# Queries and keys by Strassen's block product in the first stage of a fused attention and feed-forward kernel

## The chip, the cores and the metric

The kernel runs on one core of a Trainium2 chip, in one launch. The metric is the device time of one execution in microseconds. The profile gives, beside it, the span from the first to the last instruction of one profiled execution, which is a little shorter.

The engines: TensorE (PE; PEld is its loading of weights) multiplies, VectorE (DVE), ScalarE (ACT) and GpSimd (POOL) do the elementwise work, and SyncE (SP) issues nearly all transfers. Each has a queue of its own. SBUF is the memory on the chip, in 128 partitions; PSUM holds the matmul results, in banks of 512 float32 per partition.

## The reference

`x` is 2048 tokens by 640 features. It is normalised per token without scale or shift, and the result goes into an attention and a two-layer feed-forward part whose outputs are multiplied:

```python
xn = _layernorm(x, axis=-1)
s = _A_ref(xn, A_wqkv, A_wo)
g = _silu(_B_ref(xn, B_w1, B_b1, B_w2, B_b2))
return x + s * g
```

`_A_ref` forms queries, keys and values (`xn @ wqkv`, 640 by 1920) for 32 heads of 20 features. A token attends to itself and the 255 tokens before it, with a softmax; the outputs of all heads go through `wo`. `_B_ref` is `relu(xn @ w1 + b1)` squared, times `w2`, plus `b2`, with 1536 inner features.

## The kernel before

**High and low parts.** Every operand of a product is held as a high part in float32r, rounded by a ScalarE copy, and a low part, what the rounding left, made by a VectorE or GpSimd subtract. A product is the sum of three matmuls: high by high, low by high, high by low. The 640 features are 5 chunks of 128 (`KC`), the tokens 4 blocks of 512 (`NB`, `BT`). One group of 128 query or key features for one token block takes 5 x 3 = 15 matmuls of 512 columns.

**First stage** (L138 to L410). For each block the tokens are normalised, turned (`transpose_chunks`) and split into `xT`; the block's values are formed (`v_all`, two halves of four tiles, three banks in turn) and stored; the group-0 queries and keys of each block are formed with full matmuls (`qk_group`, L210) and stored (`qk_evac`, `qk_stores`). A stored query or key has three parts: two times the high and once the low part, so that one score matmul of 60 rows holds the three products.

**Main stage** (L1218 on). It goes through 16 head pairs with 16 key tiles each, in 267 steps. In a step, `scores` (L483) multiplies a query tile by its keys, for two heads, into the two banks of the pool `pat`; `maxima` (L491) takes row maxima with VectorE and so frees these banks; nine steps later (`LAG`) `scores_t` (L523) and `exps` (L529) make the exponentials, GpSimd masks them, and two steps after that (`PLAG`), for eight tiles together, `values` (L561) multiplies them by the values: a burst of 48 or 72 small matmuls. Between these stands the filler: a generator that hands out the remaining work a matmul at a time, as halves of 64 rows that run beside each other (L471, line L473 in the profile). Its order is: queries and keys of groups 1 to 4 for all blocks (`order_qk`, 32 products), then for two halves of the inner features and the four blocks the hidden layer (`hps`) and the second layer (`yps`), and after the last step the output product (`wops`, L627).

**What sets the order.** Both stages run under a schedule written by hand: each engine's queue takes the instructions in the order of the program, SyncE's among them, so an instruction that waits holds all behind it on its engine. In the main stage a planned clock (`COST` in microseconds for each matmul, `burst_cost`) decides how much filler stands between two steps: `total` sums all planned work, and `pace` is `total` less a surplus for the bursts, per step. `due[s]` is when step s is planned. A step does its scores, fills up to `due[s] + EARLY_FILL * pace`, and then either fills up to `due[s + 1]` or, in a burst step, runs the burst:

```python
fill(due[s] + EARLY_FILL * pace)
...
if r:
    fill(due[s + 1] - burst_cost(r))
    values(e[0], r)
else:
    fill(due[s + 1])
```

Raw weights come through a ring of three tiles (`wraw`, `RAW`), in the main stage by `piece`, `tick` and `issue`.

## Time and profile before

| | us |
|---|---|
| median of 3 runs | 843.65 (843.51 to 843.78) |
| the profiled execution | 843.45 |
| its span, first to last instruction | 841.7 |
| TensorE busy in the span | 832.2 |
| VectorE busy | 460.4 |
| ScalarE busy | 423.8 |
| GpSimd busy | 333.5 |

A row of a group in the profile names the line, the engine, the operation, what it writes and reads with shapes, and the count; then the busy time in us, the mean of one in ns, and the idle time of the engine just before them with what ended it. A piece of the chain or of the timeline has its start and its length in us. "x30" means 30 instructions merged. A matmul's own duration is longer than its distance to the next, since they are pipelined.

### The profile page before, as it was taken

To read this page: it belongs to the slowest core of one execution; us is meant where nothing else is said; L and a number is where in the kernel's file an instruction comes from. 1 tells how busy PE (TensorE), PEld (TensorE's weight loads), DVE (VectorE), ACT (ScalarE), POOL (GpSimd) and SP (SyncE) were. 2 spreads that over 40 slices of the span, in tenths; PEclk is the share of its full clock that TensorE was granted. 3 is DMA by queue.
4 is the path that set the end of the run, shared out by engine and by line. 5 is a ranking of instruction groups with operands and counts; after the bars stand their busy time and mean duration, and the time that the engine had idled before them with its cause. 6 is when DMAs were issued, how large, how long until landed. Compare 5 with 4: busy or idle time off the path is not lost.

```text
span 841.7 us, 25475 instructions
## 1 busy us (share of the span) xinstructions
PE 832.2 (99%) x10176; PEld 782.1 (93%) x10176; DVE 460.4 (55%) x1370; ACT 423.8 (50%) x792; POOL 333.5 (40%) x652
## 2 busy tenths in 40 slices
PE   8999999999999999999999999999999999999997
PEld 8999999888888999999999999899999999999997
DVE  7643126666567745455455476654445455446764
ACT  6232104545466763664653765744654755663321
POOL 5110001434333553553553553643543644552543
PEclk9999999999999999999999999999999999999999
DMA  7998488879989456345256354486365365266962
GB/s 253 288 393 331 157 205 252 267 240 278 299 267 288 144 175 176 97 163 156 80 183 193 91 147 141 125 248 197 85 223 170 83 208 189 59 187 207 385 202 79
DMA packets 89774, 166.42 MB, mean 198 GB/s; under 512 B 10424, under 2 KB 38200, under 8 KB 88632
## 3 DMA queue, kind: packets, MB, share of 16 engines
q1 hardware_dynamic: 89496, 164.64, 62.3%
q8 instruction: 80, 1.31, 0.7%
q14 instruction: 38, 0.31, 0.1%
q10 hardware_dynamic: 160, 0.16, 0.1%
HBM read 93.66 MB, written 70.52 MB: 195 GB/s over the span
## 4 chain that ended last, share of the span: by engine, by line
PE 94%; issue 1%; POOL 1%; ACT 1%; DVE 1%; DMA 1%; SPq 0%; DVEq 0%; POOLq 0%
PE yps L473 21%; PE hps L473 20%; PE qkps L473 14%; PE ops L561 10%; PE wops L627 8%; PE vps L233 8%; PE stps L523 5%; PE sps L483 4%; PE qkps L210 2%; POOL wv L189 1%; PE tps L177 1%; DMA raw<-in_A_wqkv_dram 1%; DVE junk L491 0%; ACT p L529 0%; ACT relu L977 0%
## 5 line engine op out<-in xcount | busy, mean ns | idle before, releaser
L491 DVE CUSTOM_DVE_ANT_0 junk<-sps,mask 128x384 bf16<-128x384 f32 (+2 forms) x512 | 272.3, 532 | 257.7 <-PE sps L483 81.5
L529 ACT ACTIVATE p<-stps 128x768 f32<-128x768 f32 (+2 forms) x256 | 197.4, 771 | 246.2 <-PE stps L523 202.5
L530 POOL TENSOR_SCALAR_AFFINE_SELECT p<-p 128x256 f32<-128x256 f32 x256 | 109.9, 429 | 320.5 <-ACT p L529 315.3
L473 PE MATMUL yps<-w,hh 64*128 64x320 f32 x1536 | 226.1, 309 | 0.8 <-ACT relu L977 0.8
L473 PE MATMUL hps<-xb,w 64*128 64x256 f32 (+1 forms) x2100 | 212.0, 304 | 0.0
L473 PEld LDWEIGHTS hps<-xb,w 64*128 64x128 f32 x2100 | 194.6, 187 | 3.9 <-issue 2.7
L473 PEld LDWEIGHTS yps<-w,hh 64*128 64x128 f32 x1536 | 184.2, 185 | 4.1 <-ACT relu L977 1.6
L473 PE MATMUL yps<-w,hl 64*128 64x320 f32 x768 | 175.3, 308 | 0.0
L483 PE MATMUL sps<-ks,qs 60*128 60x384 f32 (+2 forms) x512 | 132.4, 335 | 0.6 <-DVE mt L491 0.5
L523 PE MATMUL stps<-qs,ks 62*128 62x384 f32 (+2 forms) x512 | 128.0, 333 | 0.2 <-ACT row L504 0.2
L473 PEld LDWEIGHTS yps<-w,hl 64*128 64x128 f32 x768 | 117.8, 185 | 1.1 <-issue 1.0
L473 PE MATMUL qkps<-xT,wgkh 64*128 64x512 f32 x320 | 100.3, 394 | 0.0
L473 PE MATMUL qkps<-xT,wgqh 64*128 64x512 f32 x320 | 98.5, 392 | 0.0
L532 POOL TENSOR_SCALAR_AFFINE_SELECT p<-p 128x256 f32<-128x256 f32 x224 | 95.6, 427 | 0.0
L561 PE MATMUL ops<-p,vp 128*21 128x128 f32 (+1 forms) x2128 | 86.9, 311 | 0.0
L483 PEld LDWEIGHTS sps<-ks,qs 60*128 60x128 f32 x512 | 82.5, 185 | 4.6 <-DVE mt L491 2.2
L561 PEld LDWEIGHTS ops<-p,vp 128*21 128x21 f32 x2128 | 63.8, 100 | 21.2 <-issue 6.3
L523 PEld LDWEIGHTS stps<-qs,ks 62*128 62x128 f32 x512 | 81.8, 187 | 0.9 <-ACT row L504 0.6
L233 PE MATMUL vps<-wv,xT 128*128 128x320 f32 x480 | 71.9, 309 | 0.8 <-POOL wv L189 0.8
L233 PEld LDWEIGHTS vps<-wv,xT 128*128 128x128 f32 x480 | 70.5, 187 | 1.3 <-POOL wv L189 1.0
L982 POOL TENSOR_TENSOR hl<-sq,hh 128x512 fp32r<-128x512 f32 x48 | 62.1, 1294 | 16.4 <-ACT sq L981 16.3
L627 PE MATMUL wops<-wo,oT 128*128 128x320 f32 x384 | 61.9, 310 | 0.0
(104 smaller groups left out, 1167.7 us busy)
## 6 DMA issues: line engine op xcount, KB each, us to landing
ks<-k_d SPq DMA_DIRECT2D x64, 240.0 KB
qs<-q_d SPq DMA_DIRECT2D x64, 240.0 KB
xb<-xs SPq DMA_DIRECT2D x60, 256.0 KB
xs<-xT SPq DMA_DIRECT2D x8, 1280.0 KB
k_d<-shm SPq DMA_DIRECT2D x19, 512.0 KB
q_d<-shm SPq DMA_DIRECT2D x19, 512.0 KB
y<-ysb SPq DMA_DIRECT2D x28, 320.0 KB
o<-osb SPq DMA_DIRECT2D x64, 128.0 KB
```

Source lines behind the costliest of these rows:

```text
L210: nc.tensor.matmul(ps, wt[:, c, :], xT[part][b][:, c * BT + t0:c * BT + t0 + n], start=m == 1, stop=m == 3 * KC)
L233: nc.tensor.matmul(ps, xT[xp][b][:, c * BT + t * P: c * BT + (t + 1) * P], wv[wp][:, c, nh * HALF:(nh + 1) * HALF], start=first and m == 0 ...
L473: return nc.tensor.matmul(out, a[r], b_[r], skip_group_check=True, **kw)
L483: nc.tensor.matmul(ss[hh][:, :nk], qs[i][o, q * P:(q + 1) * P], ks[i][o, k0 * P:k0 * P + nk], start=True, stop=True)
L491: nc.vector.tensor_tensor_reduce(out=junk[:, :nk], in0=ss[hh][:, :nk], in1=mask[:, 3 * P - nk:], scale=1.0, scalar=-3.0e38, op0=ALU.add, o ...
L523: nc.tensor.matmul(tps[:, hh, :n], ks[i][o, kb * P:(kb + 1) * P], qs[i][o, kb * P:kb * P + n], start=True, stop=True)
L529: nc.scalar.activation(p32[:, :, :n], tps[:, :, :n], AF.Exp, scale=SCALE)
L530: nc.gpsimd.affine_select(p32[:, :, 0:P], p32[:, :, 0:P], pattern=[[0, 2], [1, P]], compare_op=ALU.is_ge, fill=0.0, base=0, channel_multip ...
L532: nc.gpsimd.affine_select(p32[:, :, 2 * P:], p32[:, :, 2 * P:], pattern=[[0, 2], [-1, P]], compare_op=ALU.is_gt, fill=0.0, base=0, channel ...
L561: nc.tensor.matmul(ot[r0:r0 + VW, c0:c0 + len(part), :], vps[p][:, kb // 4, kb % 4, hh, :], pt[:, hh, :].rearrange("p (t n) -> p t n", n=P ...
L627: nc.tensor.matmul(ps, a, b_, start=j == 0, stop=j == n - 1)
L982: nc.gpsimd.tensor_sub(hh[1][:, :BT], sq, f32(hh[0]))
```

## The change

Queries and keys of groups 1 to 4 leave the filler, and group 0 of blocks 2 and 3 leaves the first stage's direct way. They are formed in nine passes after the values. A pass takes one group of 128 features and two token blocks. The 2 by 2 block product (query and key rows by two blocks, the features cut into chunks 0, 1 and 3, 4, with chunk 2 multiplied directly) is done with seven products instead of eight, from sums of weights and sums of tokens, each split into high and low parts. The four results come from sums in the banks and copies of them.

The token sums of blocks 0 and 1 are made in `v_all(2)` by GpSimd, the first pass's weights in `v_all(3)`. In a pass, the next pass's weights, the token sums of blocks 2 and 3 (passes 1 to 4) and the rounding of the first half of `w1` (passes 5 to 7) are dealt out between the products by `aside`. The raw weights for the pass after the next are loaded at the end of a pass.

Queries and keys are stored in two parts, one store for each result, and the loads of a head pair repeat the high part: two transfers for each of the four tiles instead of one. In the main stage the filler begins with the hidden layer, with `w1`'s first half already there, and `total` has no term for queries and keys.

```diff
-    qk_d = {w: dram.tile([D, NPART, S], F32, name=f"{w}_d") for w in "qk"}
-
-    def qk_stores(w, rows, cols, hi, lo):
-        dst = qk_d[w][rows, :, cols]
-        twice, once = (slice(0, 3, 2), 1) if w == "q" else (slice(0, 2), 2)
-        return [(dst[:, twice, :], f32(hi).unsqueeze(1).to_broadcast([P, 2, hi.shape[-1]])), (dst[:, once, :], f32(lo))]
+    qk_d = {w: dram.tile([D, 2, S], F32, name=f"{w}_d") for w in "qk"}
+
+    def qk_store(w, rows, cols, both):
+        return (qk_d[w][rows, :, cols], f32(both))
...
-                r.append((f32(st[p % 2])[h * HP:h * HP + KR, cols], qk_d[w][src, :, cols].rearrange("d a n -> (d a) n")))
+                dst = f32(st[p % 2])[h * HP:h * HP + KR, cols]
+                two = qk_d["q"][src, :, cols].rearrange("d a n -> (d a) n") if w == "q" else qk_d["k"][src, 0, cols].unsqueeze(1).to_broadcast([DH, 2, HS])
+                r += [(dst[0:2 * DH], two), (dst[2 * DH:], qk_d[w][src, int(w == "k"), cols])]
...
+    PASSES = [(j, g) for j in range(2) for g in range(KC) if j or g]
+    passed, sums_of, graws = {}, {}, deque()
+
+    def load_raws():
+        k = len(graws) + len(passed)
+        if k < len(PASSES):
+            graws.append({w: load_w(group_src(PASSES[k][1], w), KC) for w in "kq"})
+
+    def weight_jobs(slots, spare):
+        k = len(passed)
+        hi, lo = ([slots(4 * a + j).rearrange("p (c n) -> p c n", n=P) for j in range(4)] for a in range(2))
...
+        raw = graws.popleft()
+        q_, k_ = raw["q"], raw["k"]
+        s14 = spare()[:, :4 * P].rearrange("p (c n) -> p c n", n=P)
+        s23 = wgt.tile([P, D], F32, tag="wraw", bufs=RAW, name="s23").rearrange("p (c n) -> p c n", n=P)
+        s1, s4 = s14[:, 0:2], s14[:, 2:4]
+
+        def rounded(j, cs, src):
+            return [lambda: nc.scalar.activation(hi[j][:, cs], src, AF.Copy), lambda: nc.gpsimd.tensor_sub(lo[j][:, cs], src, f32(hi[j][:, cs]))]
+
+        def add(dst, a, b_, sub=True):
+            return [lambda: (nc.vector.tensor_sub if sub else nc.vector.tensor_add)(dst, a, b_)]
+        cs = slice
+        return [rounded(0, cs(0, 5), q_),
+                add(s1, k_[:, 0:2], k_[:, 3:5], False),
+                rounded(1, cs(0, 3), k_[:, 2:5]),
+                add(s23[:, 0:2], s1, q_[:, 0:2]),
+                rounded(1, cs(3, 5), s1),
+                add(s23[:, 2:5], q_[:, 0:3], k_[:, 0:3]),
+                add(s4, q_[:, 3:5], s23[:, 0:2]),
+                rounded(2, cs(0, 5), s23),
+                rounded(3, cs(0, 2), s4)]
+
...
+    def token_jobs(j, tiles, mixed, room, parts):
+        sums_of[j] = t = halves_of(tiles)
...
+            one, two = part, slice(3 + part.start, 3 + part.stop)
+            (h0, l0), (h1, l1) = views
+            jobs += [op(True, 1, h1[:, one], h0[:, one]), op(False, 1, 1, l1[:, one]), op(True, 1, 1, l0[:, one]),
+                     op(True, 2, h1[:, two], 1), op(False, 2, 2, l1[:, two]), rounded(1),
+                     op(True, 4, h0[:, two], 2), op(False, 4, 4, l0[:, two]), rounded(2),
+                     op(True, 3, h1[:, two], h1[:, one]), rounded(4), op(False, 3, 3, l1[:, two]), op(True, 3, 3, l1[:, one]), rounded(3)]
+        return jobs
+
...
-            jobs = norm_jobs(b + 2) if b + 2 < NB else []
+            jobs = norm_jobs(b + 2) if b + 2 < NB else ahead_jobs[b]
...
-                    for _ in range(0 if between and not nh else 2 if between else 1):
+                    for _ in range(0 if between and not nh else 2 if between else 1 if b + 2 < NB else 2):
                         if jobs:
-                            jobs.pop(0)()
+                            run(jobs.pop(0))
...
-                for w in "kq":
-                    ps = mm_bank([P, BT], "qkps")
-                    qk_group(w, b, ps)
-                    qk_evac(w, b, ps)
+                if b == 1:
+                    for w in "kq":
+                        ps = mm_bank([P, BT], "qkps")
+                        qk_group(w, b, ps)
+                        qk_evac(w, b, ps)
                 next_x()
...
+                if b == 2:
+                    lots = [at.tile([P, S], F32R, tag=w, name=f"t_{w}") for w in ("qs0", "ks0")] + [ptt.tile([P, S], F32R, tag=f"t{i}", name=f"t_{i}") for i in range(2)]
+                    ahead_jobs[2] = token_jobs(0, lots, (), lambda: p1b.tile([P, 2, BT], F32, tag="shl", bufs=3, name="acc"), [slice(0, 2)])
+                if b == 3:
+                    ahead_jobs[3] = weight_jobs(even_slots(), lambda: p1b.tile([P, D], F32, tag="xn", name="s14"))
+                v_all(b)
+            store_all()
+            load_raws()
+
+    with tc.tile_pool(name="ph1b", bufs=1) as p1c:
+        seat = [0]
+        homes = [(pmm, "mm0"), (pmm, "mm1"), (pmm, "mm2"), (pat, "s"), (pat, "s"), (p1t, "s"), (p1t, "s"), (po_, "o")]
+
+        def bank():
+            pool, tag = homes[seat[0] % 8]
+            seat[0] += 1
+            return pool.tile([P, BT], F32, tag=tag, name="gps")
+
...
+        def copy_of(ps):
+            m = p1c.tile([P, BT], F32, tag="m", bufs=3, name="m")
+            nc.scalar.activation(m, ps, AF.Copy)
+            return m
+
+        with tc.manual_schedule(engines={E_.PE, E_.Activation, E_.DVE, E_.Pool, E_.SP}):
...
+            for i, (j, g) in enumerate(PASSES):
+                hi, lo = passed[i]
+                blocks = (2 * j, 2 * j + 1)
+                X = [[xT[p][b].rearrange("p (c n) -> p c n", c=KC) for p in range(2)] for b in blocks]
+                T = sums_of[j]
+                a, b_, c, d = (bank() for _ in range(4))
+                begun = set()
+
+                def products(ps, slot, cs, right):
+                    for n, k in enumerate(cs):
+                        for wp, xp in ((0, 0), (1, 0), (0, 1)):
+                            nc.tensor.matmul(ps, (hi, lo)[wp][slot][:, k], right(xp, n), start=id(ps) not in begun, stop=True, skip_group_check=True)
+                            begun.add(id(ps))
+
+                def rows(blk, *chunks):
+                    return lambda xp, n: X[blk][xp][:, chunks[n]]
+
+                def summed(k):
+                    return lambda xp, n: T[k][xp][:, n]
+
+                def result(w, blk, ps, m):
+                    pair = p1c.tile([P, 2, BT], F32R, tag="c", bufs=3, name="c")
+                    nc.vector.tensor_add(f32(pair[:, 1]), ps, m)
+                    nc.scalar.activation(pair[:, 0], f32(pair[:, 1]), AF.Copy)
+                    nc.vector.tensor_sub(pair[:, 1], f32(pair[:, 1]), f32(pair[:, 0]))
+                    dst, src = qk_store(w, slice(g * P, (g + 1) * P), slice(blocks[blk] * BT, (blocks[blk] + 1) * BT), pair)
+                    nc.sync.dma_start(dst, src)
+
+                def aside(n):
+                    for _ in range(n):
+                        if side:
+                            run(side.popleft())
+                if i + 1 < len(PASSES):
+                    side.extend(weight_jobs(odd_slots() if i % 2 == 0 else even_slots(), lambda: p1c.tile([P, 4 * P], F32, tag="s14", name="s14")))
+                if i == 0:
+                    lots = [p1c.tile([P, S], F32R, tag=f"t{k}", name=f"t_{k}") for k in range(4)]
+                    later_jobs = deque(token_jobs(1, lots, (4, 5, 6, 7), lambda: p1c.tile([P, 1, BT], F32, tag="acc", bufs=3, name="acc"), [slice(0, 1), slice(1, 2)]))
+                if i == KC - 1:
+                    w1_first = Tiles("w1_0")
+                    for cc in range(3):
+                        w1_load(cc)
+                    later_jobs.extend(f for cc in range(3) for f in w1_jobs(cc))
+                if i == KC:
+                    for cc in range(3, KC):
+                        w1_load(cc)
+                    later_jobs.extend(f for cc in range(3, KC) for f in w1_jobs(cc))
+                    qs.append(at.tile([P, S], F32R, tag="qs0", name="qs0"))
+                    ks.append(at.tile([P, S], F32R, tag="ks0", name="ks0"))
+                    ones_rows(0)
                     for half in range(2):
                         for dst, src in pair_loads(0, half):
                             nc.sync.dma_start(dst, src)
-                v_all(b)
-            store_all()
+                for k in range(8 if i < KC - 1 else 2):
+                    if later_jobs:
+                        side.insert(min(len(side), 1 + 2 * k), later_jobs.popleft())
+                per = -(-len(side) // 6)
+                products(a, 0, (0, 1), rows(0, 0, 1))
+                m1 = copy_of(a)
+                aside(per)
+                products(b_, 0, (3, 4, 2), rows(0, 3, 4, 2))
+                result("q", 0, b_, m1)
+                aside(per)
+                products(c, 1, (3, 4), summed(1))
+                products(c, 1, (0,), rows(1, 2))
+                m5 = copy_of(c)
+                aside(per)
+                products(a, 2, (0, 1), summed(2))
+                u2 = copy_of(a)
+                aside(per)
+                products(d, 1, (1, 2), summed(4))
+                products(d, 1, (0,), rows(0, 2))
+                aside(per)
+                products(a, 2, (2, 3), summed(3))
+                u3 = copy_of(a)
+                result("k", 0, d, u3)
+                result("k", 1, a, m5)
+                aside(per)
+                products(c, 3, (0, 1), rows(1, 3, 4))
+                products(c, 2, (4,), rows(1, 2))
+                result("q", 1, c, u2)
+                aside(len(side))
+                if i + 2 < len(PASSES):
+                    load_raws()
+            while later_jobs:
+                run(later_jobs.popleft())
...
-    total = (8 * (KC - 1) * 15 * COST[BT] + 2 * NB * (15 * (WIDE * COST[BT] + 2 * (NFH - WIDE) * COST[MT]) + 8 * 18 * COST[HALF]) + NP * 2 * NT * COST[3 * P] + sum(burst_cost(r) for p in range(NP) for r in bursts(p)))
+    total = (2 * NB * (15 * (WIDE * COST[BT] + 2 * (NFH - WIDE) * COST[MT]) + 8 * 18 * COST[HALF]) + NP * 2 * NT * COST[3 * P] + sum(burst_cost(r) for p in range(NP) for r in bursts(p)))
...
-                    assert made_for(p + 1, 0)
-                    loads = [bulk_dma(0.7, *l) for l in pair_loads(p + 1, 0)]
+                    loads = [bulk_dma(0.35, *l) for l in pair_loads(p + 1, 0)]
```

In a part left out, the first sums on `token_jobs`' list go to GpSimd, except those with the numbers in `mixed` (4 to 7 for blocks 2 and 3), which go to VectorE; `rounded` there is a ScalarE copy and a VectorE subtract. `w1_load` brings a chunk of `w1`, and `w1_jobs` rounds it with ScalarE and subtracts with VectorE.

191 lines of the change are left out of this document (92 added, 99 removed).

## The prediction

> **What bounds the kernel now.** I read the page's busy shares first, then the chain of work that ended last, then that chain in order of time.
>
> ```profile
> span 841.7 us, 25475 instructions
> PE 832.2 (99%) x10176; PEld 782.1 (93%) x10176; DVE 460.4 (55%) x1370; ACT 423.8 (50%) x792; POOL 333.5 (40%) x652
> PE 94%; issue 1%; POOL 1%; ACT 1%; DVE 1%; DMA 1%; SPq 0%; DVEq 0%; POOLq 0%
> PEclk9999999999999999999999999999999999999999
> ```
>
> TensorE is busy 99% and is 94% of the chain, at full granted clock throughout. So fewer matmuls are worth their time, as long as nothing else makes TensorE wait.
>
> ```profile
> 66.66 6.87 PE qkps L210 x30
> 93.32 6.86 PE qkps L210 x30
> 100.18 17.59 PE vps L233 x120
> 118.03 2.36 PE qkps L473 x10
> 767.28 69.87 PE wops L627 x475
> ```
>
> These pieces of the chain give the stages: the first stage ends at 117.8 us (100.18 + 17.59); attention with its filler runs to 767.3, 649.5 us; the output product follows. One 128x512 matmul costs 6.87 / 30 = 0.229 us.
>
> **The matmuls.** What goes from the main stage is 960 half matmuls, 480 whole ones:
>
> ```profile
> L473 PE MATMUL qkps<-xT,wgkh 64*128 64x512 f32 x320 | 100.3, 394 | 0.0
> L473 PE MATMUL qkps<-xT,wgqh 64*128 64x512 f32 x320 | 98.5, 392 | 0.0
> L473 PE MATMUL qkps<-xT,wgql 64*128 64x512 f32 x160 | 61.4, 392 | 0.0
> L473 PE MATMUL qkps<-xT,wgkl 64*128 64x512 f32 x160 | 61.2, 391 | 0.0
> ```
>
> Their means overlap, so I price them by the stage: the planner's own costs (COST, and `total` at L1224) sum to 628.8 for a stage that took 649.5 us, a ratio of 1.033. Its term for queries and keys is 8 x 4 x 15 x 0.23 = 110.4, so 114.0 us go (bounds: 480 x 0.229 = 109.9, and 14% of the chain, 118). From the first stage go the group-0 products of blocks 2 and 3: 6.87 + 6.86 = 13.7. What comes is nine passes. In the diff a pass has 6 + 9 + 9 + 6 + 9 + 6 + 9 = 54 matmuls of 512 columns where the direct way has 60: 12.4 us a pass, 486 x 0.229 = 111.3 in all. The balance is 111.3 - 114.0 - 13.7 = **-16.4 us**, which is all that the change can bring. The rest asks what TensorE newly waits for.
>
> **The passes.** The side engines work by these rows:
>
> ```profile
> L904 ACT ACTIVATE shm<-qkps 128x512 fp32r<-128x512 f32 x32 | 18.8, 589 | 13.8 <-PE qkps L473 12.6 <-PE sps L483 0.9
> L907 DVE TENSOR_TENSOR slo<-qkps,shm 128x512 fp32r<-128x512 f32 x32 | 22.0, 687 | 7.4 <-ACT shm L904 7.4
> L815 ACT ACTIVATE w<-raw 128x640 fp32r<-128x640 f32 x12 | 8.8, 730 | 2.6 <-DMA raw<-in_B_w_dram 2.6
> L567 ACT ACTIVATE osb<-ops 128x256 f32<-128x256 f32 x64 | 21.9, 385 | 0.0
> L189 POOL TENSOR_TENSOR wgql<-raw,wgqh 128x640 fp32r<-128x640 f32 x2 | 3.4, 1718 | 27.6 <-ACT wgqh L188 27.6
> L982 POOL TENSOR_TENSOR hl<-sq,hh 128x512 fp32r<-128x512 f32 x48 | 62.1, 1294 | 16.4 <-ACT sq L981 16.3
> ```
>
> By them ScalarE has 8 x 0.59 (four bank copies, four high parts) plus 2,176 columns of weight rounding (some 2.8) = 7.5 us of a 12.4 us pass, and VectorE 8 x 0.69 plus 1,152 columns of weight sums (some 1.6) = 7.1. They fit; order is the question, since each queue runs in program order. A result is three dependent pieces, VectorE add, ScalarE copy, VectorE subtract: 0.69 + 0.59 + 0.69, about 2.07 with the handovers. Three stand at the end of a pass in one row (k0, k1, q1). The copy that opens the row can start 1.9 us before the pass's last matmul ends and takes 0.6; so q1 is ready -1.3 + 3 x 2.07 = 4.9 us into the next pass. SyncE is in order too: it waits for q1's store, and behind that stand the loads of the two raw weights, which ScalarE needs right after the *next* pass's first bank copy. Landing times, from the SyncE issue and the ScalarE piece that a weight load released:
>
> ```profile
> 271.28 0.46 SPq L803 DMA_DIRECT2D raw<-in_B_w_dram  x1
> 275.50 0.74 ACT L815 ACTIVATE w<-raw 128x640 fp32r<-128x640 f32 x1 [1.37 <-DMA raw<-in_B_w_dram]
> 275.63 0.33 SPq L803 DMA_DIRECT2D raw<-in_B_w_dram  x1
> 278.18 0.74 ACT L815 ACTIVATE w<-raw 128x640 fp32r<-128x640 f32 x1 [1.24 <-DMA raw<-in_B_w_dram]
> ```
>
> That is 4.2 us with other transfers about and 2.6 without. I take 3.7, near the busier one, since a 512 KB store and the other weight go ahead. The query weight, second to be loaded, is issued at 4.9 + 0.4 + 0.5 = 5.8 and lands 9.5 us into the pass. Until then ScalarE stands before the rounding of that weight, and behind it stand the q0 copy, one rounding, the m5 copy, another rounding and the u2 copy: 0.73 + 0.59 + 0.5 + 0.59 + 0.39 + 0.59 = 3.4 us. The u2 copy must have read bank `a` before its third products, due after 39 matmuls, at 8.9 us. TensorE waits 9.5 + 3.4 - 8.9 = 4.0 us. Seven passes (the second to the eighth) load so: **+28** (20 to 32 by the two landings; 0 if ScalarE gets there earlier than I count).
>
> The first four passes also carry the token sums of blocks 2 and 3 (12 GpSimd pieces of about 1.29 us, 16 VectorE and 8 ScalarE pieces), and passes five to seven the rounding of the first half of w1. A ScalarE piece that waits for a chain of GpSimd sums holds the next bank copy. Nothing before shows this order, so I bound it. In the first pass GpSimd needs 1.7 + 1.0 for two weight remainders and 3 x 1.29 for the first sum after the raw weight lands; VectorE's next sum and, behind a weight sum, ScalarE's next rounding stand behind that, so u3 comes some 5 us late and with it the second pass's raw weights; fading over three passes, 11 us. A w1 piece puts some 0.8 of ScalarE and a VectorE subtract ahead of q0: 3 to 4 a pass, 10 in all. The ends are 0, if the sums run ahead, and 21; I take **+10**, the middle. GpSimd has 2,176 columns a pass (5.5 us) and 12 x 1.29 / 4 of sums, 9.4 together.
>
> Two engines that read the same memory slow each other in this trace:
>
> ```profile
> 742.08 0.41 POOL L530 TENSOR_SCALAR_AFFINE_SELECT p<-p 128x256 f32<-128x256 f32 x1 [1.79 <-ACT p L529]
> 744.13 0.92 POOL L530 TENSOR_SCALAR_AFFINE_SELECT p<-p 128x256 f32<-128x256 f32 x1
> 743.19 2.53 DVE L825 TENSOR_TENSOR wo<-raw,wo 128x640 fp32r<-128x640 f32 x2 [0.76 <-ACT wo L824]
> ```
>
> The same select takes 0.41 us alone and 0.92 beside VectorE subtracts of two SBUF operands. [...]
>
> **Before the passes.** In the value products of block 2, GpSimd gets ten token sums of 1,024 columns, about 2.5 us each (2 x 1.29). It can begin only behind the memset that waits for a store:
>
> ```profile
> 70.91 0.24 POOL L241 MEMSET vt<- 128x64 f32 x1 [11.77 <-DMA v_d<-vt]
> ```
>
> From 71.2 they end near 96.4. ScalarE's rounding of the last sum (about 1.0) stands ahead of its copy of the block's last value bank, which is then read at 97.8. That bank is due for the third tile of the next value block, at (100.18 - 13.7) + 2 x 2.2 = 90.9 (17.59 / 8 = 2.2 a tile). I take **+6**, 0 to 7 being the ends.
>
> **The main stage.** The same scores now stand between 110 us fewer matmuls. The planner's `pace` falls from (628.8 - 30.3) / 266 = 2.25 to (518.4 - 30.3) / 266 = 1.83 a step. In a step with a burst of value products, scores come first, then work up to 0.4 pace, then the burst (2.81); the step is due at pace + 1.01. So it ends 0.4 x 2.25 + 2.81 - 3.26 = 0.45 late and the next step has 1.80. The trace has it:
>
> ```profile
> 372.84 2.75 PE ops L561 x72
> 375.53 0.44 PE L483 MATMUL sps<-ks,qs 60*128 60x384 f32 x1
> 377.30 0.34 PE L483 MATMUL sps<-ks,qs 60*128 60x384 f32 x1
> 377.60 0.33 PE L483 MATMUL sps<-ks,qs 60*128 60x384 f32 x1
> 376.15 0.56 DVE L491 CUSTOM_DVE_ANT_0 junk<-sps,mask 128x384 bf16<-128x384 f32 x1 [2.36 <-PE yps L473]
> 376.86 0.56 DVE L491 CUSTOM_DVE_ANT_0 junk<-sps,mask 128x384 bf16<-128x384 f32 x1
> 377.35 0.08 DVE L491 DVE_READ_ACCUMULATOR2_ANT mt<- 128x1 f32 x1
> ```
>
> 375.53 to 377.30 is 1.77. VectorE, idle before, finishes the second maximum at 377.43, and the next step's second score, which reuses that bank, starts at 377.60: 0.17 to spare. With pace 1.83 the step ends 0.70 late and the next has 1.14. 0.66 less makes TensorE wait 0.49, 0.52 with the handover, in each of 30 bursts (two in each of 15 head pairs): **+15.6**. Below, 0 if other waits spread the steps; above, 20. In other steps two maxima and their reads (1.3 us) leave 0.5 of 1.83, and a VectorE piece that meets them eats it; I take **+5**, 0 to 15. ScalarE's exponentials, 0.81 each, have the same step and wait at the same place.
>
> What I cost at nothing: the third stored part (10 MB less; no store is on the chain; SyncE's issues are shorter); twice as many pair loads, 16 issues of about 0.4 in a pair of some 33 us, cover gone only if the loads of a pair outlast the pair before; the loads of pair 0 in the sixth pass, ahead of that pass's stores, covered by three result tiles (if not, up to 4 us); the rounding of w1's first half, gone from ScalarE and VectorE in the main stage; the value bursts and the row maxima, which the planner already keeps two and five steps behind what they need.
>
> **Sum** against the profiled execution's own time, 843.45 (span 841.7; the median shown is 843.65, the same within 0.03%): 843.45 - 16.4 + 28 + 10 + 6 + 15.6 + 5 = 891.65, **892 us**, +5.7%.
>
> **The rivals.** *TensorE's floor* (faster). The raw weights land within 5.5 us of a pass's start (8.9 - 3.4), as they would if q1's result did not hang on the whole row, and the burst's short step is stretched by other filler. Then 843.45 - 16.4 = 827, up to 838 with small waits. For it: 99% busy now and side engines at 40 to 55%. Against: q1 cannot be stored before its matmuls end, and 0.17 us is all the slack after a burst. It decides when all waits together are under 14.7 us. Chance 0.15; 0.03 for a time within 0.2%, which is about what a measurement of this kernel can tell from no change. *Passes clean, bursts wait*: 843.45 - 16.4 + 20.6 = 848, 846 to 855; 0.17. *All covers gone*: 28 to 32 for the loads, 21 for the sums, 7 before them, 35 in the main stage: 843.45 - 16.4 + 95 = 922; 905 to 930; 0.22. The forecast's own case, 856 to 905: 0.43. That the matmul count does not fall is excluded by the diff.
>
> [...] The granted clock is full in every slice now, where TensorE never idles for more than a moment. [...]
>
> **Chances and range.** Faster 0.15, same 0.03, slower 0.82. 844 to 920 leaves out the floor and the top of the worst case, some 0.2.
>
> **What would show it.** Right: 54 `gps` matmuls a pass, passes of 16 to 18 us instead of 12.4, TensorE waiting for the ScalarE line of the bank copies, ScalarE idle for the DMA of `raw`; the product tiles of the last value block waiting for a late bank; after each burst a score waiting for L491, and fewer microseconds between steps. Wrong: passes of 12.4 us with no wait, raw weights that land early, or TensorE still busy 99%. If GpSimd's sums ran long before they are needed, the +10 and +6 go; if the step after a burst kept its length, the 15.6 goes.

## The result and the profile after

The changed kernel takes 975.46 us (median of 4 runs, 973.49 to 975.98), the kernel before 843.71 beside it: 1.156 times as long, with a 95% interval of 1.154 to 1.158. The prediction said slower, 892, at most 920; it is slower by 132 us instead of 48. The profiled execution took 973.49 us, its span 971.8.

From the page of the changed kernel, the lines that answer to those shown of before: span, busy shares, granted clock in 40 slices, the chain that ended last.

```profile
span 971.8 us, 24791 instructions
PE 864.2 (89%) x9642; PEld 787.5 (81%) x9642; DVE 533.0 (55%) x1451; ACT 469.1 (48%) x877; POOL 423.8 (44%) x717
PEclk9998987777778799999999999999999999999999
PE 56%; DVE 5%; DMA 5%; ACT 2%; issue 2%; SPq 1%; DVEq 0%; ACTq 0%
```

TensorE was busy 99% of 841.7 us and is now busy 89% of 971.8. Its 534 fewer matmuls are as the diff has them, but it idles for 107.6 us (971.8 less 864.2), and in slice 4 and slices 6 to 14 its clock falls to 0.7 and 0.8. The same table by stretches (length, busy time and count of each engine, granted clock, DMA share, GB/s) shows where: the end of the first stage, the nine passes, the main stage.

```profile
core 0: us, PE busy (x) PEld busy (x) DVE busy (x) ACT busy (x) POOL busy (x), PEclk, DMA share, GB/s
60.00:113.55 53.55, 47.70 (x306) 46.77 (x304) 22.73 (x31) 13.30 (x25) 32.78 (x19) 0.90 0.42 153
113.55:126.50 12.95, 12.68 (x55) 10.17 (x56) 4.15 (x4) 3.55 (x7) 5.59 (x5) 1.00 0.49 146
126.50:159.50 33.00, 17.23 (x56) 13.24 (x55) 19.02 (x22) 10.37 (x19) 16.16 (x12) 0.74 0.26 83
...
234.99:258.74 23.75, 15.13 (x56) 11.97 (x55) 10.80 (x16) 8.63 (x16) 5.95 (x5) 0.78 0.73 231
...
282.49:302.99 20.50, 15.26 (x56) 12.02 (x55) 9.52 (x14) 6.85 (x13) 6.06 (x5) 0.83 0.41 135
302.99:315.35 12.36, 12.36 (x56) 9.94 (x54) 4.19 (x7) 4.69 (x8) 0.00 (x0) 1.00 0.45 170
315.35:896.90 581.55, 555.95 (x7986) 511.05 (x7985) 333.33 (x1139) 344.97 (x656) 277.91 (x592) 0.99 0.50 152
```

Only the first and the last pass take the 12.4 us that 54 matmuls need; the last is the one with no load behind it. The others take 20.5 to 33.0, and no side engine is busy for 60% of that. Set beside the prediction's terms:

| stretch | by matmuls alone | predicted | measured |
|---|---|---|---|
| first stage up to the passes (117.8 - 13.7) | 104.1 | 110 | 113.55 |
| nine passes | 111.3 | 149.3 | 201.8 |
| main stage (649.5 - 114.0) | 535.5 | 556 | 581.5 |
| output product and end | 74.4 | 74.4 | 74.9 |

Of the some 82 us that the prediction is short, 52 lie in the passes, 25 in the main stage, 4 ahead of the passes. Who waits for whom in the passes (the view of waits, all engines: engine and line, releaser, us in total, times, the longest):

```profile
PE gps L561 <- ACT m L525: 68.8, 10, 12.3
...
ACT wgkh L171 <- DMA raw<-in_A_wqkv_dram: 28.6, 4, 8.0
...
ACT aw L171 <- DMA raw<-in_A_wqkv_dram: 22.3, 4, 7.5
```

All of TensorE's idle time in the passes but 0.5 us is the wait for ScalarE's copy of a bank, and ScalarE's longest waits are for the raw weights. The eighth pass (it starts at 282.49) has this chain alone, with neither sums nor w1. From the timeline (start, length, engine, line, operation; in brackets the idle time before and what ended it):

```profile
286.04 0.51 SPq L576 DMA_DIRECT2D q_d<-c  x1
286.65 1.67 SPq L149 DMA_DIRECT2D raw<-in_A_wqkv_dram  x2
292.71 0.43 DVE L174 TENSOR_TENSOR s<-raw 128x256 f32<-128x256 f32 x1 [6.70 <-DMA raw<-in_A_wqkv_dram]
293.74 0.74 ACT L171 ACTIVATE wgkh<-raw 128x640 fp32r<-128x640 f32 x1 [7.97 <-DMA raw<-in_A_wqkv_dram]
...
294.55 1.53 POOL L171 TENSOR_TENSOR wgkh<-raw,wgkh 128x640 fp32r<-128x640 f32 x1 [15.23 <-ACT wgkh L171]
...
295.03 1.60 DVE L574 TENSOR_TENSOR c<-c 128x512 fp32r<-128x512 f32 x1 [1.29 <-ACT c L573]
...
296.10 0.58 ACT L525 ACTIVATE m<-gps 128x512 f32<-128x512 f32 x1
```

SyncE issues the store of q1 3.55 us into the pass and the two loads behind it at 4.2. VectorE and ScalarE get the weights 6.1 and 7.1 us after the first issue, the second of them 11.25 us into the pass. From there ScalarE needs 2.94 us to the end of its copy of bank `a` (296.68). TensorE, which had done 39 matmuls 9.0 us into the pass, goes on at 14.25. The chain that ended last, in order of time, has the same:

```profile
287.30 6.36 DMA raw<-in_A_wqkv_dram
296.74 16.66 PE gps L561 x60
```

In the main stage TensorE's longest wait ends 8.5 us behind the stage's start, for a score that waits for VectorE's first maximum:

```profile
323.47 0.29 DVE L716 CUSTOM_DVE_ANT_0 junk<-sps,mask 128x128 bf16<-128x128 f32 x1 [3.25 <-DMA q_d<-c]
323.83 1.02 PE L708 MATMUL sps<-ks,qs 60*128 60x256 f32 x2 [4.93 <-DVE mt L716]
```

VectorE's maximum writes `junk`, a scratch tile whose memory had held a result tile `c` of the last pass, and that is still being stored.

### The profile page after: what moved, and what is told of

Its sections match the earlier page's. It is cut to its first block, busy times and chain, and to the rows that moved or that the text cites. A ratio compares the mean times of both kernels' runs of the same rounds, so it can differ in the third digit from the quotient of the medians.

```text
span 971.8 us, 24791 instructions
## 1 busy us (share of the span) xinstructions
PE 864.2 (89%) x9642; PEld 787.5 (81%) x9642; DVE 533.0 (55%) x1451; ACT 469.1 (48%) x877; POOL 423.8 (44%) x717
## 4 chain that ended last, share of the span: by engine, by line
PE 56%; DVE 5%; DMA 5%; ACT 2%; issue 2%; SPq 1%; DVEq 0%; ACTq 0%
PE yps L698 15%; PE hps L698 15%; PE ops L786 8%; PE wops L852 7%; PE sps L708 5%; DVE junk L716 4%; PE stps L748 4%; PE gps L561 2%; DMA qs<-q_d 1%; DMA qs<-mrow 1%; DMA raw<-in_A_wqkv_dram 1%; SPq L921 1%; DMA o<-osb 1%; DMA ks<-k_d 1%; ACT c L573 1%
## 5 line engine op out<-in xcount | busy, mean ns | idle before, releaser
L698 PE MATMUL yps<-w,hh 64*128 64x320 f32 x1536 | 234.9, 311 | 2.2 <-DVE ysb L1158 1.3
L698 PE MATMUL hps<-xb,w 64*128 64x256 f32 (+1 forms) x2100 | 222.1, 305 | 0.0
L698 PEld LDWEIGHTS hps<-xb,w 64*128 64x128 f32 x2100 | 201.1, 186 | 3.5 <-issue 3.1
L698 PEld LDWEIGHTS yps<-w,hh 64*128 64x128 f32 x1536 | 192.2, 186 | 6.9 <-issue 2.7
L698 PE MATMUL yps<-w,hl 64*128 64x320 f32 x768 | 183.7, 310 | 0.0
L708 PE MATMUL sps<-ks,qs 60*128 60x384 f32 (+2 forms) x512 | 138.0, 350 | 13.8 <-DVE mt L716 13.4
L698 PEld LDWEIGHTS yps<-w,hl 64*128 64x128 f32 x768 | 124.0, 186 | 1.3 <-issue 1.2
L748 PEld LDWEIGHTS stps<-qs,ks 62*128 62x128 f32 x512 | 75.5, 187 | 11.2 <-issue 8.9
L852 PEld LDWEIGHTS wops<-wo,oT 128*128 128x128 f32 x384 | 57.6, 188 | 0.2 <-issue 0.2
L561 PE MATMUL gps<-t,aw 128*128 128x512 f32 x72 | 23.9, 483 | 35.3 <-ACT m L525 35.3
```

The lines of the kernel that those rows point to most:

```text
L561: nc.tensor.matmul(ps, (hi, lo)[wp][slot][:, k], right(xp, n), start=id(ps) not in begun, stop=True, skip_group_check=True)
L698: return nc.tensor.matmul(out, a[r], b_[r], skip_group_check=True, **kw)
L708: nc.tensor.matmul(ss[hh][:, :nk], qs[i][o, q * P:(q + 1) * P], ks[i][o, k0 * P:k0 * P + nk], start=True, stop=True)
L748: nc.tensor.matmul(tps[:, hh, :n], ks[i][o, kb * P:(kb + 1) * P], qs[i][o, kb * P:kb * P + n], start=True, stop=True)
L852: nc.tensor.matmul(ps, a, b_, start=j == 0, stop=j == n - 1)
```

## The experiments

The two theories at the start: the passes are long because the raw weights stand behind q1's store in SyncE's order (the prediction's step, mis-sized); or because the side engines have too much to do, or do it in a bad order, so that the loads are only where the waiting shows. Each kernel was run once beside the kernel before, which took 843.19 to 844.98. How far single executions differ shows in the stages that an edit leaves alone: over these kernels the same first stage ends at 111.1 to 113.6 us, the same passes take 200.0 to 201.8 (157.6 and 159.9 with early loads), and the same main stage 581.2 to 589.5. A difference inside these bounds shows nothing.

**1. No load** (e1). From the third pass on the weights of the second are used again; in a part left out the tile of weight sums, `s23`, is one tile for all passes instead of a turn in the ring.

```diff
-            graws.append({w: load_w(group_src(PASSES[k][1], w), KC) for w in "kq"})
+            if k < 2:
+                kept.append({w: load_w(group_src(PASSES[k][1], w), KC) for w in "kq"})
+            graws.append(kept[-1])
```

> Leaves out the raw weight loads of the third to ninth pass: all later weights are formed from the second pass's raw tiles, so the output differs. Theory (ScalarE, in order, stands before a raw weight that is still on its way, and the bank copies TensorE needs stand behind it): the waits after 39 matmuls go, passes fall from 20 to 27 us to 12.4 to 15, the nine passes from 202 to 115 to 130 us, the whole to 885 to 905. Rival (the side engines are simply full: GpSimd and VectorE excluding each other, token sums, w1): passes stay above 17 us and the whole above 935.

**2. Loads earlier** (e2). All is computed; `load_raws` stands ahead of the last three results instead of behind them.

```diff
                 aside(per)
+                if i + 2 < len(PASSES):
+                    load_raws()
                 products(a, 2, (2, 3), summed(3))
...
                 aside(len(side))
-                if i + 2 < len(PASSES):
-                    load_raws()
```

> The raw weight loads of a pass are issued before its last two stages instead of behind q1's store. Theory: they leave some 5 us earlier against the next pass and land near the time ScalarE needs them; passes of 13 to 18 us, the nine 125 to 165 us, the whole 900 to 940. Rival (side engines full): within 10 us of 975.

Without loads 931.74 us, with earlier ones 928.67; the passes take 160.1 and 157.6 instead of 201.8. So it isn't the transfer that costs, but its place: loads issued ahead of the three results' stores cost nothing more. That is 44 us, and 46 are left over the 111.3 of the matmuls. So both theories hold a part: the time of e1 lies between what the one and the other expected. In e2 the wait for the bank copies (view of waits, passes) falls to half:

```profile
PE gps L561 <- ACT m L525: 33.0, 10, 6.6
```

**3. The clock kept up** (e3). 36 more matmuls stand where TensorE waits, low by low parts added to bank `d`, which changes k0 in its low parts.

```diff
+                if 0 < i < len(PASSES) - 1:
+                    for n in range(36):
+                        nc.tensor.matmul(d, lo[1][:, 1 + n % 2], T[4][1][:, n % 2], start=False, stop=True, skip_group_check=True)
                 products(a, 2, (2, 3), summed(3))
```

> 36 more matmuls (low by low part, into the bank of k0) stand before the waiting products in passes two to eight, so TensorE is busy while it would wait. Clock theory (the long wait halves the granted clock, and the 15 matmuls after it take 6.2 us instead of 3.4): the clock stays at 1.0, a pass loses 2 to 3 us, the whole comes to 950 to 960. Rival (those matmuls are slow because of what the other engines do then): no gain, 975 or more.

978.83 us, of which the main stage, which the edit leaves alone, takes 589.5 (why 8 more stays open). The passes of e3 by windows, beside 0.81 and 133.00 us of TensorE in the changed kernel:

```profile
113.40:312.60 199.20, 176.19 (x738) 141.59 (x738) 94.55 (x123) 67.87 (x124) 67.78 (x52) 0.96 0.42 137
```

The clock is 0.96, and the last 15 matmuls of a pass take 3.4 to 3.5 us instead of 5.9 to 6.3, except in the fourth pass, which still waits 5.1 us and then takes 5.8 for them; the third products of the seventh pass, from the timeline, first changed kernel, then e3:

```profile
276.25 2.92 PE L561 MATMUL gps<-t,wgkl 128*128 128x512 f32 x6 [8.52 <-ACT m L525]
```

```profile
262.67 1.68 SPq L149 DMA_DIRECT2D raw<-in_A_wqkv_dram  x2
268.98 0.74 ACT L171 ACTIVATE aw<-raw 128x640 fp32r<-128x640 f32 x1 [7.18 <-DMA raw<-in_A_wqkv_dram]
276.35 1.66 PE L561 MATMUL gps<-t,wgkl 128*128 128x512 f32 x6 [2.65 <-ACT m L525]
```

So the clock follows the waits, but restoring it gives back only 2.6 us of the passes' 201.8, hardly more than single executions differ, where seven times 2.6 would be 18. The second and fifth pass get 2.7 us shorter, the third and fourth 1.4 longer, and the sixth and seventh take 23.69 and 23.67 as against 23.75: the load of the seventh is issued at 262.67 instead of 263.08 and releases ScalarE at 268.98 instead of 268.92. There the loop of load, rounding, copy, results and store sets the pass, and faster matmuls hardly shorten it: the loads of the seventh and the eighth pass are issued 0.4 and 1.2 us earlier. In the eighth pass the 36 matmuls take longer than its wait, and e3 tells nothing.

**4. Filler in the main stage** (e4): `EARLY_FILL = 0.1` instead of 0.4, so that filler moves from ahead of a burst to behind it, between the two scores that share a bank.

> EARLY_FILL 0.4 becomes 0.1: less filler between the scores and a burst, so the step after a burst keeps 1.6 us of plan instead of 1.14. Theory (the score after a burst waits for VectorE's second maximum, 0.5 us in each of 30 bursts): the main stage loses 10 to 14 us of its 581, the whole comes to 960 to 966. Rival (the main stage is longer for other reasons, such as VectorE and ScalarE being fuller in every step): no gain or a loss.

963.33 us; the main stage takes 575.4 instead of 581.5, the median head pair 32.8 instead of 33.4. That the whole lies within the expected 960 to 966 is partly luck: the main stage gives 6 us of the 10 to 14, and the rest lies in stages that the edit leaves alone. TensorE's waits for the maxima fall from 13.4 to 9.7 us; those for the row maxima's stores, at which the edit does not aim, fall from 7.9 to 3.1. The bursts are a cause, then, but a small one, of which 3.7 us are shown.

**5. What else is in the passes** (f1, f2). f1 is e2 without the 20 token sums a part of blocks 2 and 3; f2 is e2 with the rounding of w1 six places later in the list of side work, and the loads of the first head pair two passes later. The first diff is that of f1 (`j` is 1 for these blocks), the second that of f2.

```diff
+                    if j:
+                        acc.setdefault(k, views[0][0][:, part])
+                        return
```

```diff
-                        side.insert(min(len(side), 1 + 2 * k), later_jobs.popleft())
+                        side.insert(min(len(side), 1 + 2 * k + (6 if i >= KC - 1 else 0)), later_jobs.popleft())
...
+                if i == len(PASSES) - 2:
                     for half in range(2):
```

> On the kernel with the early loads (928.67 us, nine passes 157.6 us). Leaves out the 20 sums a part of the tokens of blocks 2 and 3; their roundings stay, from single blocks, so the output differs. Theory (with the loads early, what is left in passes two to four is the chain of GpSimd sums that ScalarE and VectorE stand before): passes two to four fall from 23.5, 18.2 and 22.8 to 12.4 to 14.5, the nine to 128 to 137, the whole to 900 to 910. Rival (the weight sums and roundings alone overfill VectorE and GpSimd): these passes stay above 17, the whole above 918.

> On the kernel with the early loads. The rounding of w1 is dealt out behind the u2 copy instead of ahead of q0, and the loads of head pair 0 go from the sixth pass to the eighth. Theory (in passes five to seven ScalarE and VectorE stand before w1 pieces, and SyncE's pair loads hold the stores): these passes fall from 20.2, 14.6 and 20.7 to 12.4 to 15, the whole to 910 to 918. Rival (these passes are late from the token passes before them): less than 5 us gained.

f1: 913.38 us, passes 140.5; the sums are worth 17 us. Of the passes that the theory names the third falls to 12.3, as it had it, but the second and the fourth only to 17.4 and 17.1, and the whole misses the 900 to 910: the sums are not all that is left there. f2: 924.30 us, passes 153.4. The fifth to seventh pass fall to 12.3, 14.2 and 14.3, as the theory had it, but the ninth rises from 12.3 to 22.0, since it now waits 7.0 us after 24 matmuls. So the whole gains 4.4 us, within the rival's 5, though not for the rival's reason. f2's timeline:

```profile
247.30 0.76 SPq L602 DMA_DIRECT2D qs<-q_d  x2
248.79 0.56 SPq L576 DMA_DIRECT2D q_d<-c  x1
254.28 0.69 DVE L572 TENSOR_TENSOR c<-gps,m 128x512 f32<-128x512 f32 x1 [7.06 <-DMA q_d<-c]
```

The moved head-pair loads hold SyncE until 248.1, the store of a result behind them is late, and VectorE waits for that result's tile to come free. Both at once, run later as h2:

> e2 (raw weights loaded earlier) with both remedies at once: the 20 token sums a part of blocks 2 and 3 left out as in f1 (its output lacks them), and the rounding of w1 behind the pass's copies as in f2. Passes 157.6 in e2, 140.5 without the sums, 153.4 with the late rounding. Theory: the two costs stand in different passes and add up, the sums 17 and w1 some 14 of which the last pass gives 10 back: 135 to 138, of which passes 4 to 6 take under 14.5 each. Rival: they cover one another: 139 to 141. What is then left over 111.3 is the order of the three results at a pass's end.

911.46 us, passes 135.4: they add up, as the theory had it, but the fourth and the sixth pass stay at 15.3 and 17.6 where it had under 14.5. The ninth pass has 9.6 us too many here as well; in the rest 14.5 us over the matmuls are left, most of them in the second, fourth and sixth pass, each with one wait of 2.7 to 3.5 us.

**6. The first stage** (h1): the changed kernel without the ten sums of blocks 0 and 1.

```diff
+                    if not j:
+                        acc.setdefault(k, views[0][0][:, part])
+                        return
```

> The changed kernel with the ten token sums of blocks 0 and 1 on GpSimd left out (its output lacks them); their rounding on ScalarE and VectorE stays. The first stage took 113.55 us before the passes began, 9.5 more than 104.0, the time without the change less its 13.7 us of products. Theory: GpSimd's sums (69.7 to 96.7) hold VectorE's and ScalarE's value copies, and the matmuls after that wait run at half clock: first stage 104 to 106. Rival: the new loads or the roundings hold it: over 109. The passes stay at 200 to 202.

964.33 us. From its windows (one row), against the first row of the changed kernel's windows above:

```profile
60.00:104.40 44.40, 43.87 (x305) 43.60 (x304) 17.45 (x31) 13.18 (x25) 6.34 (x9) 1.00 0.49 177
```

Without these sums GpSimd is busy 26.4 us less and the passes begin at 104.4 instead of 113.55, at full clock instead of 0.90; the passes still take 201.7. Beside all kernels with the same first stage (111.1 to 113.6) the gain is 6.7 to 9.1 us. The term is what the prediction took it for, and somewhat larger than its 6. In the changed kernel's timeline:

```profile
89.77 2.35 DVE L214 TENSOR_TENSOR t<-acc,t 128x1024 fp32r<-128x1024 f32 x1 [3.37 <-ACT t L214]
...
92.04 0.48 DVE L360 COPY vt<-vps 128x320 f32<-128x320 f32 x1
92.57 4.37 PE L335 MATMUL vps<-wv,xT 128*128 128x320 f32 x15 [4.02 <-DVE vt L360]
96.81 1.06 ACT L214 ACTIVATE t<-acc 128x1024 fp32r<-128x1024 f32 x1 [7.08 <-POOL acc L209]
97.77 0.42 ACT L358 ACTIVATE vt<-vps 128x320 f32<-128x320 f32 x1
```

ScalarE's rounding of the last sum holds its bank copy until 97.8, exactly as worked out. What I left out: behind the sum before, VectorE's subtract of 2.35 us holds its own bank copy until 92.0, and the 15 matmuls behind that wait take 4.37 us instead of some 2.2.

**7. The start of the main stage** (f3, f4, g1). f3 is e2 with `junk` in memory of its own.

```diff
-junk = at2.tile([P, 3 * P], BF16, tag="junk", bufs=1, name="junk")
+junk = const.tile([P, 3 * P], BF16, tag="junk", name="junk")
```

> On the kernel with the early loads. VectorE's scratch tile of the maxima lies in memory that no tile of the passes used. Theory (the main stage's first maximum writes over a result tile of the last pass and waits for its store to land, 3.3 us, TensorE 4.9 us behind it at half clock): the main stage starts 4 to 9 us sooner, the whole 920 to 925. Rival (another reused tile or a load holds the start just as long): no gain.

933.29 us, no gain: the second score no longer waits, but one some steps later does, 5.7 us (at 288.39). f3's timeline:

```profile
286.19 0.74 ACT L1023 ACTIVATE w<-raw 128x640 fp32r<-128x640 f32 x1 [10.42 <-DMA raw<-in_B_w_dram]
286.96 0.89 DVE L1026 TENSOR_TENSOR w<-raw,w 128x384 fp32r<-128x384 f32 x2 [6.67 <-ACT w L1023]
```

ScalarE and VectorE stand before the first piece of w2, with the maxima behind them. In the program its load stands where the stage begins (271.6), but SyncE issues it at 282.63, 11.0 us later: ahead of it in the queue are the last result's store, at 276.96, and a load of values (L649) that waits for that store to land. From the view of SyncE's waits:

```profile
SPq L649 <- DMA q_d<-c: 4.4, 1, 4.4
```

It is a store ahead of the loads once more, and no kernel here moves it. f4 puts all remedies together: earlier loads, late w1 rounding and head-pair loads, `junk` apart, four of ten first sums on VectorE, k0 and k1 interleaved, `EARLY_FILL` 0.1, the term for the bursts' surplus 1.5 instead of 1.8, and blocks 2 and 3 by 60 direct matmuls (so 24 matmuls saved instead of 54).

> All remedies together: early loads, late w1, pair loads late, scratch tile apart, four of ten sums of blocks 0 and 1 on VectorE, k0 and k1 interleaved, EARLY_FILL 0.1 and a longer due step for bursts, and blocks 2 and 3 by 60 direct matmuls a pass instead of 54 (six passes' worth of side work less, 7 us more of TensorE). If the causes named are all there are, the passes take 118 to 125 us, the first stage ends at 106 to 111, the main stage takes 555 to 568, the whole 853 to 880. If something else holds the passes or the main stage, over 890.

880.77 us, just over the 853 to 880 expected. The passes take 117.9, at their floor (516 matmuls x 0.229 = 118.2): no wait over 0.5 us is left in them, though five of the nine are direct now. The first stage ends at 109.5, as expected; the main stage takes 576.7, well over the 555 to 568. g1 is f4 with the first w2 pieces rounded eight steps after their load instead of two:

```diff
-            if not force and (tag in shut or state[2] < at_ + AGE):
+            if not force and (tag in shut or state[2] < at_ + (AGE if at_ > 3 else 8)):
...
-        if not started or started[0][0] in shut or state[2] < started[0][1] + AGE:
+        if not started or started[0][0] in shut or state[2] < started[0][1] + (AGE if started[0][1] > 3 else 8):
```

> f4 with one line more: the pieces of w2 whose loads are issued in the first four steps of the main stage are rounded eight steps later instead of two. In f4 the fifth score step waited 3.54 us for VectorE's maximum; VectorE had stood 4.28 us before the subtract of a w2 piece, which waited for ScalarE's high part, which waited for the load of `raw`. Theory: the start of the main stage loses its time to that row of waits alone, now that the scratch tile lies apart; main stage 576.7 - 5 = 570 to 573, no score of the first twelve steps waits over 1 us. Rival: as with the scratch tile alone, the wait only moves to the next load in line (the inputs of the two-layer part or the results of the last pass): 575 to 578.

877.13 us, the best of all these kernels and still 4% slower than before; 1.9 of the 3.6 us less than f4 lie in the first stage, which the edit leaves alone. The score waits fall from 5.9 us (longest 3.5) in f4 to 2.9 (longest 0.5), TensorE's waits in g1's main stage being these:

```profile
PE stps L780 <- DMA qs<-mrow: 5.4, 5, 1.6
PE yps L730 <- DVE ysb L1190: 3.1, 5, 1.2
PE sps L740 <- DVE mt L748: 2.9, 10, 0.5
```

But the stage only falls from 576.7 to 575.0, no more than single executions differ, and the first burst still starts 45.6 us after the first score (45.8 in f4, 42.0 before the change). The first load of w2 is still issued 10.8 us into the stage. So the wait had the cause that the theory named, but hardly the price: the rival was nearer in the time.

**8. The row maxima** (g2): g1 with their stores issued by GpSimd's queue instead of SyncE's.

```diff
-                nc.sync.dma_start(f32(qs[i])[KR + a:KR + a + HP + 1:HP, g * BT:(g + 1) * BT].rearrange("h (q n) -> h q n", q=4), f32(mrow)[:, a, :])
+                nc.gpsimd.dma_start(f32(qs[i])[KR + a:KR + a + HP + 1:HP, g * BT:(g + 1) * BT].rearrange("h (q n) -> h q n", q=4), f32(mrow)[:, a, :])
```

> g1 with the negative row maxima stored by GpSimd's queue instead of SyncE's, where 16 loads of the next head pair and other transfers stand ahead of them. In f4 TensorE waited 5.92 us in six places for these stores. Theory: that wait is SyncE's order; it goes, main stage 4 to 6 us below g1. Rival: the maxima themselves come late (ScalarE's copy, GpSimd's remainder) or GpSimd's queue is as late: within 2 us of g1.

902.80 us, main stage 599.1. The wait does not go, it grows:

```profile
PE stps L780 <- DMA qs<-mrow: 19.9, 17, 2.3
```

The theory was wrong, by its sign, and the rival too. Of the 24 us that the main stage grows, this wait has 14.5; the rest stays open. Whether SyncE's order makes that wait isn't shown by this; only that the other queue is no remedy.

## Why the prediction was right in sign and wrong in size

The steps that failed are sizes of terms, and for the token sums and w1 the fading by which theirs was got; the waits of the passes were the ones foretold. In the passes the raw weights cost 44 us instead of 28, and the token sums and w1 31.8 instead of 10, taken away in this order, and 14.5 more were not taken apart: these make the 52 us. In the main stage the waits for the maxima are smaller than the sum had them, and what makes its 25 us is a floor 6.6 us higher, waits for stores that were put at nothing, and matmuls that follow one another more slowly.

**Matmuls, -16.4.** Right for the passes: 54 `gps` matmuls each, 12.36 to 12.95 us where nothing waits. For the main stage I took 114.0 by the planner's ratio; the timeline of before, summed over the starts of its `qkps` matmuls, gives 107.4, so its floor is 649.5 - 107.4 = 542.1 and the change could have brought 9.8 us, not 16.4. The bound of 109.9 by the first row was the nearer one.

**Raw weights, +28.** The mechanism was right to the step: loads behind q1's store, ScalarE before the rounding of that weight, a wait at the 40th matmul. Taken away alone (e2) it gives 44 us, 6.3 a pass instead of 4.0. The mis-sized term is the landing: I took 3.7 us from rows of a 320 KB load of whole rows; two weights in pieces of 512 bytes, behind 512 KB stores, took 6.4. The chain of before has a load of the very same shape, at the kernel's start, with 4.76 us, which was the nearer row:

```profile
2.18 4.76 DMA raw<-in_A_wqkv_dram
```

The other estimates were on the safe side (second issue at 4.8 instead of 5.8, ScalarE's work 2.9 instead of 3.4 us), so that the eighth pass waits 5.2 us for 4.0; and its last 15 matmuls, at a granted clock of 0.53 (296.74 to 302.99), which the sum left out, take 2.8 more.

**Token sums and w1, +10 (0 to 21).** The step that failed most. By taking away, in this order: sums 17.1 us (e2 to f1); w1, together with the pair loads moved out of the sixth pass, 5.1 and the 9.6 that h2 gives back in the ninth pass. That is 31.8 us, outside my bounds. Another 14.5 remain in h2's other passes over 111.3; what they are made of was not taken apart: in f4 they are gone, but it changes the order of the results and makes five passes direct at once. I bounded each piece by its own delay, once, and let it fade; but a late copy makes late results, a late store and late loads in the next pass, so each pass begins behind. A w1 piece shows it: ScalarE's two stand ahead of the bank copies, after a load that is already late (fifth pass, changed kernel):

```profile
222.33 0.74 ACT L171 ACTIVATE aw<-raw 128x640 fp32r<-128x640 f32 x1 [7.54 <-DMA raw<-in_A_wqkv_dram]
223.31 0.84 ACT L541 ACTIVATE w<-w1raw 128x768 fp32r<-128x768 f32 x1 [0.24 <-DMA w1raw<-in_B_w_dram]
224.19 1.31 DVE L548 TENSOR_TENSOR w<-w1raw,w 128x768 fp32r<-128x768 f32 x1 [9.16 <-ACT w L541]
226.72 0.83 ACT L541 ACTIVATE w<-w1raw 128x768 fp32r<-128x768 f32 x1
227.45 0.58 ACT L525 ACTIVATE m<-gps 128x512 f32<-128x512 f32 x1
```

I had used the busy sums (7.5 of 12.4 us on ScalarE) as a sign that "they fit". ScalarE's do fit, in every pass (10.4 at most). VectorE's don't: it is busy 19.0 us in the second pass, and 49.3 in the first four together, which take 49.4 by their matmuls. So in these passes the other theory, too much to do, has a part; but in f1 the second still takes 17.4 us with VectorE busy 11.3, so the order counts there too. In the later passes everything fits but the chain through three queues.

VectorE and GpSimd slow each other in the passes too. VectorE's subtract of 512 columns takes 0.69 us alone (281.29 in the changed kernel) and 1.60 beside GpSimd (295.03 above, beside a GpSimd subtract at 294.55); GpSimd's subtract of 384 columns takes 1.45 beside VectorE (296.05) where the shortest of that shape took 0.99. What this costs in the first four passes the runs do not show: f1's 17 us are the sums' own time and the slowing together.

**The clock.** In before it is full in every slice, and the sum has no term for it. After, it is 0.74 to 0.83 over the second to the eighth pass, whose longest waits are 5.2 to 12.3 us, and 0.50 from 276.25 to 282.05, behind the 8.5 us of the seventh. As a slowing of matmuls that is some 2.6 us a pass, 18 in seven; as a price it was far less in e3, whose passes got 2.6 us shorter in all with the clock at 0.96. What it costs in the eighth pass stays open.

**Before the passes, +6 (0 to 7).** 6.7 to 9.1 by h1: right engine and bank, a second bank left out, and the granted clock of 0.50 in the 15 matmuls behind it (92.57 to 97.00).

**The burst's step, +15.6, and other steps, +5.** The mechanism is there but smaller. After a burst the second score of the next step waits for VectorE, 0.27 us at 398.19:

```profile
393.77 2.58 PE L786 MATMUL ops<-p,vp 128*21 128x256 f32 x60
396.29 0.44 PE L708 MATMUL sps<-ks,qs 60*128 60x384 f32 x1
396.62 0.34 PE L708 MATMUL sps<-ks,qs 60*128 60x384 f32 x1
397.48 0.44 PE L708 MATMUL sps<-ks,qs 60*128 60x384 f32 x1
398.19 0.44 PE L708 MATMUL sps<-ks,qs 60*128 60x384 f32 x1 [0.27 <-DVE mt L716]
```

In the whole stage TensorE waits 13.4 us in 33 places for these maxima, of which 4.9 are the start; 8.5 are left for bursts and other steps instead of 20.6, and e4 took 3.7 of the 13.4 away. Main stage 581.5 over 542.1 is 39.4, and TensorE idles for 25.6 of them: these 13.4, 7.9 for the row maxima's stores in three places (I had costed them at nothing), and the rest in small pieces. Some 5 are matmuls at a lower clock at both ends of the stage (0.65 up to 330 us; 0.91 from 875 to 895), an estimate from the busy time there. The other 9 or so stay open: matmuls that follow one another more loosely without a wait that the trace names. They are the filler: from start to start, less the idle time, its 4,704 matmuls of the hidden and the second layer take 370.2 us, the lower clock's share among them, and took 354.2 before. In g1, with idle waits down to 16 us, the stage still takes 575.0.

**The loads of the first head pair, 0, and the stage's start.** What the main stage meets at its start is what the last pass leaves behind: a scratch tile in memory still being stored, and w2 loads that stand behind that store in SyncE's order. Both were shown as waits (f3, g1), but neither's removal shortened the main stage by more than 2 us. That the loads of the first head pair can be in the way showed in f2 and h2, with 9.6 us where I had set up to 4.

**The rivals.** All covers gone (905 to 930) had the largest sum and was the nearest, still 45 us short; its sums had the landing and the bounds above in them. The floor was excluded, and not by one wait: under 14.7 us of waits in all would have been needed, and TensorE idled 107.6.

## What to carry to other kernels

In queues in program order, look for the loop, not for the busiest engine: here store, load, rounding, copy, result and store again set a pass of 20 to 33 us with every side engine under 60% busy, and moving two loads ahead of three stores gave 44 us. But take busy sums pass by pass: a mean of all hides the one pass that is too full (VectorE was busy 19.0 us in the second, whose matmuls take 12.4). Take a landing time from a row of the same shape of transfer with the same company, and when there is none, let the range reach far. A term that returns in each pass of a loop is not to be faded out: what is late at the end of a pass is the start of the next.

## What the runs showed of the hardware that I had not expected

Behind waits of 5.2 to 12.3 us, at the end of the second to the eighth pass, 15 matmuls took 5.9 to 6.3 us instead of 3.4, with the granted clock at 0.52 to 0.57 over them (0.50 from 276.25 to 282.05), and other matmuls in the waits kept it at 0.96 over the passes (e3). Two weights loaded as 512-byte pieces behind a store of 512 KB take 6.4 us to land where a 320 KB load took 2.6 to 4.2. 128 small stores moved from SyncE's to GpSimd's queue made the kernel 26 us slower (877.13 to 902.80); each takes GpSimd about 0.55 us to issue, and TensorE's wait for them went from 5.4 to 19.9 us.
